# A spectral mixer and a low-rank MLP mixer on one core: output stores of 128 rows, V by broadcast loads, px two pairs ahead

## The chip, the cores and the metric

The kernel runs on one core of a Trainium2 chip. The metric is the device time of one execution in microseconds (us). Four compute engines work side by side, each through its own instructions in order: TensorE (PE in the profile, its weight loads PEld), VectorE (DVE), ScalarE (ACT) and GpSimd (POOL). SyncE (SP) only issues transfers. Transfers are issued here from POOL's queue and from SP's queue, and all of them are carried by 16 DMA engines.

## The reference

The input `x` has 8 batches of 3136 rows with 256 channels. Cut to what matters:

```python
X = np.fft.rfft(x, axis=1)
y = np.fft.irfft(X * (filt_r + 1j * filt_i)[None], n=3136, axis=1)   # global filter over the rows
yt = y.transpose(0, 2, 1)
u = y + (yt @ U @ V).transpose(0, 2, 1)          # U: 3136 x 32, V: 32 x 3136
out = u + np.maximum(u @ w_ch1, 0.0) @ w_ch2     # 256 -> 1024 -> 256, for every row
```

Inputs and output are float32. Inside, the kernel works in float16 with float32 sums.

## The kernel before, in words

**The transform.** 3136 = 64 x 49, so a row number is 49 q + r. The Fourier transform over q (64 points) is a product with the matrix `w64`, the one over r with the tables `t2`. What comes out of `t2`, the tile `px`, is multiplied by the filter tile `ft`; the tables `g12` take the result back over r, giving the spectrum `e2` over q alone, which stays as it is until the MLP needs it. The work of one batch in the middle stage is 16 pairs m of 64-row frequency groups: `forward` (L382) makes `px`, `both_products` (L390) or `product` (L401, L403) multiplies by the filter into `uv`, and a third step goes back over r.

**Batch 0** takes a way of its own, without DRAM in the middle: `first_f1` (L255 to L271), `first_a` (L283, L285) and `first_mid` (L294 to L337). In the loop of `first_mid`, pair m's `px` is made right before its product; the PSUM tag "m", from which it takes its bank, has 4 banks. At the loop's first round of a quarter, `swap_filters` (L188, L189) copies a quarter of the filter to the other half of the partitions and negates the imaginary part. After the loop, transposes (L328) fill `e2`, and between them run the first steps of batch 1, `f1_units`.

**Batches 1 to 7** go through DRAM between the steps. `f1_units` (L348) multiplies a chunk of `x` by `w64` and copies it to a tile `asb`, of which there are 3; each chunk is stored to `c1` (L358) by two transfers, from SP for batch 1 and from POOL for the others. `load_a` (L367) reads it back by frequency, `stream` runs the 16 pairs and stores `esb` to `c2` (L424), and `load_e` (L374) reads that into `e2`.

**The low rank part.** `U` and `V` are brought into the kernel's order. V is loaded in `load_v` (L210) by four loads that each fill 32 partitions of a constant tile `vq`; `prep_v` (L215) reorders it to `vr` by two GpSimd copies. `h1_unit` (L449) makes U's product `ph`, copied to `h1` (L453). `make_u` (L471, L476, L501) then adds V's product and brings the spectrum back to rows.

**The MLP and the output.** Rows are dealt with in groups: a group is up to 4 values of r, each with 128 rows (64 of r and 64 of r + 25). Each batch has 6 groups of 4; the values r = 24 of two batches share one short group, with one value, after every odd batch. `mm1` (L508) and `mm2` (L529, L533) are the two layers of a group, and mm2 of a group runs beside mm1 of the next. DVE copies the sums to the output tile `och` (L538), of which there are 2, two values of r at a time. After a group's last copy, two stores of 64 partitions each go to the output from POOL's queue (L545).

**What sets the order.** The order on every engine is the order in which the program writes its instructions. A table `sched` written out by hand (`put`, `run`) names slots in the groups' sequence at which the steps of later batches are written between the matmuls; a batch takes 48 slots, two for each quarter of a group of 4. Tiles of one tag share a given number of buffers: the writer of a tile waits until the tile that held its buffer before is read. Each new load of `x` waits for one of 8 `xt` buffers.

Of the kernel before, what the change touches and what calls it, by code (L numbers as in the profile page):

```python
# [9 lines left out]
F16 = mybir.dt.float16  # L10
F32 = mybir.dt.float32
RELU = mybir.ActivationFunctionType.Relu

SEQ = 3136
NQ, NR = 64, 49
NS = 32
DM = 256
RANK = 32
ESC = 16.0
NH = 25  # L20
CH = [6, 6, 6, 7]
# [64 lines left out]
def kernel(  # L86
# [40 lines left out]
    def rows(ap, b, o, n, np_=NQ):  # L127
        return bass.AP(tensor=ap.tensor, offset=ap.offset + b * SEQ * DM + o,
                       ap=[[RD, np_], [1, n]])
# [65 lines left out]
        load_filters(a, b)  # L195
    uq = sb.tile([64, NR * RANK], F16, tag="esb", bufs=2, name="uq")
    nc.gpsimd.dma_start(uq, moe_U.rearrange("(q r) p -> q (r p)", q=NQ))
    vq = cst.tile([128, SEQ], F16)
    w1 = cst.tile([128, 2 * 1024], F16)
    nc.gpsimd.dma_start(w1, moe_w_ch1.rearrange("(h dd) c -> dd h c", h=2))  # L200
    w2 = cst.tile([128, 8 * DM], F16)
# [3 lines left out]
    vr = cst.tile([128, NH * 128], F16)  # L205
    usb = cst.tile([128, NH * RANK], F16)

    def load_v():
        for j in range(4):
            nc.gpsimd.dma_start(vq[32 * j:32 * j + 32, :], moe_V)  # L210

    def prep_v():
        for h in range(2):
            w = NH - h
            nc.gpsimd.tensor_copy(  # L215
                vr.rearrange("p (r h q) -> p h r q", h=2, q=NQ)[:, h, 0:w, :],
                vq.rearrange("p (q r) -> p r q", r=NR)[:, h * NH:h * NH + w, :])

    def new_e2(b):
        e2 = sb.tile([128, NH * DM], F16, tag="e2", bufs=2, name="e2")  # L220
# [53 lines left out]
    def first_a(m):  # L274
        gi, ml = divmod(m, KG // 2)
        if ml == 0:
            st[0].setdefault("a", {})[gi] = sb.tile([98, KG * DM], F16, tag="a2", bufs=4, name="a2")
        pt = bank("o", "pt")
        for sl in range(2):
            for dh in range(2):  # L280
                o = sl * DM + dh * 128
                k = dh * 64 * NR + (2 * m + sl) * 98
                nc.tensor.matmul(pt[0:98, o:o + 128], at[:, k:k + 98], idn[:, :],  # L283
                                 start=True, stop=True, skip_group_check=True)
        nc.scalar.copy(st[0]["a"][gi][:, ml * 512:(ml + 1) * 512], pt[0:98, :])  # L285


    def first_mid(fill):

        et = sb.tile([128, 2 * NH * 128], F16, tag="e2", bufs=2, name="et")  # L290
        etv = et.rearrange("p (e r h k) -> p h e r k", e=2, h=2, k=64)
        pend = None

        def back(m, uv):  # L294
            pi = bank("fx"[m % 2], "pi")
            for sl in range(2):
                for dh in range(2):
                    for fi in range(2):
                        g = (4 * m + 2 * sl + fi) * 98
                        o = fi * 512 + sl * DM + dh * 128  # L300
                        a = (dh * 2 + sl) * 98
                        nc.tensor.matmul(pi[:, a:a + 98], uv[:, o:o + 128], g12[:, g:g + 98],
                                         start=(fi == 0), stop=(fi == 1), skip_group_check=True)
            for h in range(2):
                nc.scalar.copy(
                    etv[:, h, :, 0:NH - h, 4 * m:4 * m + 4],
                    pi[:, 0:392].rearrange("p (e k r) -> p e r k", e=2, r=NR)
                    [:, :, h * NH:h * NH + NH - h])

        for m in range(NS // 2):  # L310
            if m % 4 == 0 and m:
                swap_filters(*PARTS[m // 4])
            uv = both_products(m, forward(m, st[0]["a"][m // 4], ("m",)))
            if pend is not None:
                back(*pend)
            pend = (m, uv)
            if m + 2 < NS // 2:
                first_a(m + 2)
        back(*pend)
        e2 = new_e2(0)  # L320
        for n0 in range(0, NH, 2):
            pt = bank("m", "pe")
            w = min(2, NH - n0)
            k = 64 if w == 1 else 128
            for rr in range(w):
                for dh in range(2):
                    o, a = rr * DM + dh * 128, (dh * NH + n0 + rr) * 128
                    nc.tensor.matmul(pt[0:k, o:o + 128], et[:, a:a + k], idn[:, :],  # L328
                                     start=True, stop=True, skip_group_check=True)
            dst = e2[0:k, n0 * DM:(n0 + w) * DM]  # L330
            if n0 % 4:
                nc.scalar.copy(dst, pt[0:k, 0:w * DM])
            else:
                nc.vector.tensor_copy(dst, pt[0:k, 0:w * DM])
            if n0 == 6:
                prep_u()
            next(fill)  # L337

    def f1_units(b, both):
        ne = 0  # L340
        for c in range(len(CH)):
            xt = st[b]["x"].pop(c)
            asb = sb.tile([128, 7 * DM], F16, tag="asb", bufs=3, name="asb")
            for n0 in range(0, CH[c], 2):
                w = min(2, CH[c] - n0) * DM
                k = 64 if c0[c] + n0 == NH - 1 else 128
                pf = bank("m", "pf")
                nc.tensor.matmul(pf[0:k, 0:w], w64[0:k, 0:k], xt[0:k, n0 * DM:n0 * DM + w],  # L348
                                 start=True, stop=True)
                dst = asb[0:k, n0 * DM:n0 * DM + w]  # L350
                if both and ne % 2:
                    nc.vector.tensor_copy(dst, pf[0:k, 0:w])
                else:
                    nc.scalar.copy(dst, pf[0:k, 0:w])  # L354
                ne += 1
                if n0 + 2 >= CH[c]:
                    for h, o, n in span(c0[c], c0[c + 1]):
                        (nc.sync if b == 1 else nc.gpsimd).dma_start(c1[b].ap()[:, o:o + n], asb[64 * h:64 * h + 64, 0:n])  # L358
                yield
# [17 lines left out]
    def forward(m, a2, xtags):  # L377
        ml = m % (KG // 2)
        px = bank(xtags[m % len(xtags)], "px")
        for sl in range(2):  # L380
            s = 2 * m + sl
            nc.tensor.matmul(px[:, sl * DM:(sl + 1) * DM], t2[:, s * 128:(s + 1) * 128],  # L382
                             a2[:, (2 * ml + sl) * DM:(2 * ml + sl + 1) * DM],
                             start=True, stop=True, skip_group_check=True)
        return px

    def both_products(m, px):
        uv = sb.tile([128, 1024], F16, tag="uv", bufs=3, name="uv")
        fap = ft[:, 2 * m * DM:2 * (m + 1) * DM]
        nc.vector.tensor_mul(  # L390
            uv.rearrange("p (f e) -> p f e", f=2),
            bass.AP(tensor=px.tensor, offset=px.offset, ap=[px.ap[0], [0, 2], [1, 512]]),
            bass.AP(tensor=fap.tensor, offset=fap.offset,
                    ap=[fap.ap[0], [NS * DM, 2], [1, 512]]))
        return uv
# [121 lines left out]
    def mm2(gx, rr):  # L517
        if gx < 0 or rr >= groups[gx][2]:
            return
        b, r0, nr = groups[gx]  # L520
        w = nr * 128
        if rr == 0:
            ochs[gx] = sb.tile([128, 4 * DM], F32, tag="och", bufs=2, name="och")
        if rr % 2 == 0:
            pos[gx] = bank("o", "po")
        po, ut, och = pos[gx], uts[gx], ochs[gx]
        o = (rr % 2) * DM
        for t in range(8):
            nc.tensor.matmul(po[:, o:o + DM], hs[gx, t][:, rr * 128:(rr + 1) * 128],  # L529
                             w2[:, t * DM:(t + 1) * DM], start=(t == 0), stop=False,  # L530
                             skip_group_check=True)
        for dh in range(2):
            nc.tensor.matmul(po[:, o + dh * 128:o + (dh + 1) * 128],  # L533
                             ut[:, dh * w + rr * 128:dh * w + (rr + 1) * 128], idn[:, :],
                             start=False, stop=(dh == 1), skip_group_check=True)
        if rr % 2 or rr == nr - 1:
            a = (rr - rr % 2) * DM
            nc.vector.tensor_copy(och[:, a:(rr + 1) * DM], po[:, 0:(rr + 1) * DM - a])  # L538
        if rr == nr - 1:
            for h in range(2):  # L540
                if nr == 1:
                    dst = rows(out, b - 1 + h, r0 * DM, DM)
                else:
                    dst = rows(out, b, (h * NH + r0) * DM, nr * DM)
                nc.gpsimd.dma_start(dst, och[64 * h:64 * h + 64, 0:nr * DM])  # L545

    sched = {}

# [13 lines left out]
    for part in PARTS[1:]:  # L562
        load_tables(*part)
    swap_filters(*PARTS[0])
    first_a(0)
    first_a(1)
    for b in (1, 2):
        for c in range(len(CH)):
            load_x(b, c)
        if b == 1:  # L570
            load_v()
    fill = f1_units(1, True)
    first_mid(fill)
    prep_v()
    next(h1_unit(0))
    make_u(0)

# [72 lines left out]
```

## Time and profile before

| | us |
|---|---|
| median of 3 runs (575.88 to 576.89) | 576.33 |
| the profiled execution | 578.7 |
| its span, from the first instruction to the last | 576.7 |
| TensorE busy in it | 529.6 |
| DVE, ACT, POOL busy | 371.3, 359.8, 250.7 |

The mean granted TensorE clock was 0.976. How to read the profile: a group line gives the source line, engine, operation, and written and read tile, with the count, the busy time and the mean; in the timeline a line begins with its start from the span's beginning and its duration, and the bracket at its end is the engine's idle time just before it and what ended that. In the DMA view a queue's line gives its packets, megabytes and the time its packets took as a share of 16 engines' time; an issue line gives the count, the size of each and the median time from issue to landing. A packet here is one contiguous piece that a DMA engine moves, or one of the small end marks that tell of a transfer's end. All times of steps come from the one profiled execution.

### The profile page before, as it was taken

How to read it: one execution, taken by the hardware profiler on the slowest of the kernel's cores; microseconds unless marked ns; L12 is line 12 of the kernel's file. 1: busy time of each engine (PE TensorE's matmuls, PEld its weight loads, DVE VectorE, ACT ScalarE, POOL GpSimd, SP SyncE). 2: the span in 40 equal slices, each digit the busy share in tenths (PEclk: the TensorE clock that was granted, in tenths of full speed). 3: DMA queues.
4: the chain of work that ended last, by engine and by line, in shares of the span. 5: the costliest groups of instructions: out<-in, count | busy, mean ns of one | idle time of the engine just before them, and what ended most of it. 6: DMA issues, size and time to landing. Idle time of an engine off the chain costs nothing.

```text
span 576.7 us, 11509 instructions
## 1 busy us (share of the span) xinstructions
PE 529.6 (92%) x4403; PEld 376.4 (65%) x4403; DVE 371.3 (64%) x544; ACT 359.8 (62%) x723; POOL 250.7 (43%) x356
## 2 busy tenths in 40 slices
PE   3666899999999999999999999999999899999990
PEld 3553467767677767767676767777777577677770
DVE  7886276766777577767777578767777477233440
ACT  3566656667667586667677686777665466644430
POOL 6546340254556456455555455454443443110111
PEclk9989799999999999999999999999999899999996
DMA  8999758876978857677879857777564654512221
GB/s 153 216 184 223 212 129 179 179 194 149 201 189 207 186 132 165 157 192 199 185 169 206 210 123 185 170 159 206 133 166 108 155 116 98 130 42 70 73 73 47
DMA packets 68150, 90.40 MB, mean 157 GB/s; under 512 B 6728, under 2 KB 53224, under 8 KB 67200
## 3 DMA queue, kind: packets, MB, share of 16 engines
q0 software_dynamic: 19664, 51.88, 40.9%
q1 hardware_dynamic: 48432, 37.81, 26.8%
q8 instruction: 34, 0.56, 0.4%
q14 instruction: 20, 0.16, 0.1%
HBM read 57.99 MB, written 48.17 MB: 184 GB/s over the span
## 4 chain that ended last, share of the span: by engine, by line
PE 80%; DVE 2%; ACT 2%; DMA 1%; issue 1%; POOL 0%; POOLq 0%; DVEq 0%; ACTq 0%
PE po L529 29%; PE phh L508 28%; PE pi L418 5%; PE px L382 4%; PE pu L471 4%; PE po L533 4%; PE pu L476 4%; PE pf L348 2%; ACT h L515 2%; DMA out_dram<-och 1%; DVE uv L403 1%; PE ph L449 1%; DVE uv L401 1%; DVE uv L390 0%; POOL out_dram L545 0%
## 5 line engine op out<-in xcount | busy, mean ns | idle before, releaser
L515 ACT ACTIVATE h<-phh 128x512 f16<-128x512 f32 (+1 forms) x350 | 186.6, 575 | 108.0 <-PE phh L508 107.5
L529 PE MATMUL po<-w,h 128*128 128x256 f16 x1568 | 203.2, 273 | 0.0
L508 PE MATMUL phh<-ut,w 128*128 128x512 f16 x768 | 198.5, 380 | 0.4 <-ACT ut L501 0.2
L406 POOL TENSOR_TENSOR y<-uv 128x512 f16<-128x512 f16 x96 | 110.3, 1149 | 150.8 <-DVE uv L403 76.8
L529 PEld LDWEIGHTS <-h 128*128 128x128 f16 x1568 | 150.1, 98 | 35.7
L403 DVE TENSOR_TENSOR uv<-px,ft 64x512 f16<-64x512 f32 x192 | 132.1, 688 | 2.6
L538 DVE COPY och<-po 128x512 f32<-128x512 f32 (+1 forms) x100 | 68.1, 681 | 88.5 <-PE po L533 79.6
L508 PEld LDWEIGHTS <-w 128*128 128x128 f16 x832 | 75.2, 98 | 53.0 <-issue 3.3
L545 POOL DMA_DIRECT2D out_dram<-och x104 | 55.8, 540 | 113.3 <-DVE och L538 103.5
L401 DVE TENSOR_TENSOR uv<-px,ft 128x512 f16<-128x512 f32 x96 | 66.0, 688 | 56.0 <-PE px L382 49.7
L422 ACT CAST esb<-pi 98x512 f16<-98x512 f32 x112 | 65.8, 588 | 43.2 <-PE pi L418 35.5
L382 PE MATMUL px<-a,t 98*128 98x256 f16 x256 | 51.2, 282 | 5.7 <-DVE uv L403 4.3
L354 ACT CAST asb<-pf 128x512 f16<-128x512 f32 (+1 forms) x79 | 44.9, 569 | 17.8 <-PE pf L348 15.7
L501 ACT CAST ut<-pu 128x512 f16<-128x512 f32 x96 | 52.0, 597 | 4.8 <-PE pu L476 4.5
L533 PE MATMUL po<-idn,ut 128*128 128x128 f16 x384 | 52.8, 219 | 0.0
L513 DVE TENSOR_SCALAR h<-phh 128x512 f16<-128x512 f32 (+1 forms) x66 | 42.9, 650 | 14.3 <-PE phh L508 13.8
L390 DVE TENSOR_TENSOR uv<-px,ft 128x1024 f16<-128x1024 f32 x32 | 38.5, 1221 | 10.2 <-PE px L382 9.8
L476 PEld LDWEIGHTS <-e 128*128 128x128 f16 (+1 forms) x400 | 31.7, 99 | 19.6 <-issue 4.7
L471 PE MATMUL pu<-vr,h 128*128 128x512 f16 (+1 forms) x112 | 40.6, 362 | 2.6 <-POOL vr L215 1.7
L476 PE MATMUL pu<-s,e 128*128 128x128 f16 (+1 forms) x400 | 41.2, 222 | 0.0
L533 PEld LDWEIGHTS <-ut 128*128 128x128 f16 x384 | 37.6, 98 | 4.4
L134 POOL DMA_DIRECT2D xt<-in_x_dram x64 | 34.3, 543 | 9.0 <-DMA w<-in_moe_w_ch_dram 3.6
(66 smaller groups left out, 348.1 us busy)
## 6 DMA issues: line engine op xcount, KB each, us to landing
out_dram<-och POOLq DMA_DIRECT2D x96, 256.0 KB, 4.2
a<-c SPq DMA_DIRECT2D x28, 392.0 KB
c<-esb SPq DMA_DIRECT2D x28, 392.0 KB
xt<-in_x_dram POOLq DMA_DIRECT2D x56, 192.0 KB, 6.2
c<-asb POOLq DMA_DIRECT2D x42, 192.0 KB, 3.2
e<-c SPq DMA_DIRECT2D x28, 200.0 KB
e<-c SPq DMA_DIRECT2D x28, 192.0 KB
xt<-in_x_dram POOLq DMA_DIRECT2D x8, 224.0 KB, 5.1
```

The source lines that it names most:

```text
L382: nc.tensor.matmul(px[:, sl * DM:(sl + 1) * DM], t2[:, s * 128:(s + 1) * 128], a2[:, (2 * ml + sl) * DM:(2 * ml + sl + 1) * DM], start=Tru ...
L401: nc.vector.tensor_mul(uv[:, 0:512], px[:, :], ft[:, a:a + 512])
L403: nc.vector.tensor_mul(uv[p:p + 64, 512:1024], px[q:q + 64, :], ft[q:q + 64, b:b + 512])
L406: nc.gpsimd.tensor_add(y, uv[:, 0:512], uv[:, 512:1024])
L422: nc.scalar.copy(esb[:, ml * 512:(ml + 1) * 512], pi[0:98, :])
L471: nc.tensor.matmul(pm[:, o:o + nr * k], h1[:, dh * 128:(dh + 1) * 128], vr[:, r0 * 128:r0 * 128 + nr * k], start=True, stop=False, skip_gr ...
L476: nc.tensor.matmul(pm[:, o + rr * k:o + (rr + 1) * k], e2[0:k, a:a + 128], s2[0:k, 0:k], start=False, stop=(rr == nr - 1), skip_group_chec ...
L508: nc.tensor.matmul(pm[:, 0:w], w1[:, dh * 1024 + t * 128:dh * 1024 + (t + 1) * 128], ut[:, dh * w:(dh + 1) * w], start=(dh == 0), stop=(dh ...
L515: nc.scalar.activation(h[:, 0:w], pm[:, 0:w], RELU)
L529: nc.tensor.matmul(po[:, o:o + DM], hs[gx, t][:, rr * 128:(rr + 1) * 128], w2[:, t * DM:(t + 1) * DM], start=(t == 0), stop=False, skip_gr ...
L533: nc.tensor.matmul(po[:, o + dh * 128:o + (dh + 1) * 128], ut[:, dh * w + rr * 128:dh * w + (rr + 1) * 128], idn[:, :], start=False, stop= ...
L538: nc.vector.tensor_copy(och[:, a:(rr + 1) * DM], po[:, 0:(rr + 1) * DM - a])
```

## The change

- **Stores.** A group's two stores of 64 partitions become one store of 128 partitions. Its DRAM side has the dimensions [2][64][row], its SBUF side is the tile's 128 partitions. Batches 0 to 6 issue it from POOL, the last batch from SP. The short group's tile is of a tag of its own, `ocho`, with one buffer.
- **V.** Two loads, one for each half of V's columns, each with a leading dimension of 4 with stride 0, fill 128 partitions. They use the two buffers of the tag `och`, which is free then, and the constant tile `vq` goes. They are issued before the loads of the MLP's weights, and the loads of x for batch 1 follow them directly. `prep_v` becomes 8 pieces of two copies, written before `first_mid`, with a load of x for batch 2 after every second one.
- **px.** In the loop of `first_mid` the `px` of pairs m + 1 and m + 2 are made before the product of pair m needs them, and `first_a` runs three pairs ahead instead of two.
- **asb.** It has 4 buffers instead of 3.

```diff
@@ loads at the start
-    vq = cst.tile([128, SEQ], F16)
+    vqs = [sb.tile([128, SEQ // 2], F16, tag="och", bufs=2, name="vq") for _ in range(2)]
+    for k in range(2):
+        nc.gpsimd.dma_start(vqs[k], bass.AP(
+            tensor=moe_V.tensor, offset=moe_V.offset + k * (SEQ // 2),
+            ap=[[0, 4], [SEQ, RANK], [1, SEQ // 2]]))
+    for c in range(len(CH)):
+        load_x(1, c)
     w1 = cst.tile([128, 2 * 1024], F16)
...
-    def load_v():
-        for j in range(4):
-            nc.gpsimd.dma_start(vq[32 * j:32 * j + 32, :], moe_V)
-
-    def prep_v():
+    def prep_v(k):
+        q0, n = 8 * k, 8
+        v = vqs[k // 4]
+        a = (q0 % (NQ // 2)) * NR
         for h in range(2):
             w = NH - h
             nc.gpsimd.tensor_copy(
-                vr.rearrange("p (r h q) -> p h r q", h=2, q=NQ)[:, h, 0:w, :],
-                vq.rearrange("p (q r) -> p r q", r=NR)[:, h * NH:h * NH + w, :])
+                vr.rearrange("p (r h q) -> p h r q", h=2, q=NQ)[:, h, 0:w, q0:q0 + n],
+                v[:, a:a + n * NR].rearrange("p (q r) -> p r q", r=NR)[:, h * NH:h * NH + w, :])
@@ first_mid
+        def ahead(m):
+            return forward(m, st[0]["a"][m // 4], ("m",))
+
+        pxs = [ahead(0), ahead(1)]
         for m in range(NS // 2):
             if m % 4 == 0 and m:
                 swap_filters(*PARTS[m // 4])
-            uv = both_products(m, forward(m, st[0]["a"][m // 4], ("m",)))
+            uv = both_products(m, pxs.pop(0))
             if pend is not None:
                 back(*pend)
             pend = (m, uv)
             if m + 2 < NS // 2:
-                first_a(m + 2)
+                pxs.append(ahead(m + 2))
+            if m + 3 < NS // 2:
+                first_a(m + 3)
@@ f1_units
-            asb = sb.tile([128, 7 * DM], F16, tag="asb", bufs=3, name="asb")
+            asb = sb.tile([128, 7 * DM], F16, tag="asb", bufs=4, name="asb")
@@ mm2
-            ochs[gx] = sb.tile([128, 4 * DM], F32, tag="och", bufs=2, name="och")
+            ochs[gx] = (sb.tile([128, 4 * DM], F32, tag="och", bufs=2, name="och") if nr > 1 else
+                        sb.tile([128, DM], F32, tag="ocho", bufs=1, name="ocho"))
...
-            for h in range(2):
-                if nr == 1:
-                    dst = rows(out, b - 1 + h, r0 * DM, DM)
-                else:
-                    dst = rows(out, b, (h * NH + r0) * DM, nr * DM)
-                nc.gpsimd.dma_start(dst, och[64 * h:64 * h + 64, 0:nr * DM])
+            o, step = ((b - 1) * SEQ, SEQ) if nr == 1 else (b * SEQ, NH)
+            dst = bass.AP(tensor=out.tensor, offset=out.offset + (o + r0) * DM,
+                          ap=[[step * DM, 2], [RD, NQ], [1, nr * DM]])
+            (nc.gpsimd if b < nb - 1 else nc.sync).dma_start(dst, och[:, 0:nr * DM])
@@ the order of the start
-    first_a(0)
-    first_a(1)
-    for b in (1, 2):
-        for c in range(len(CH)):
-            load_x(b, c)
-        if b == 1:
-            load_v()
+    for m in range(3):
+        first_a(m)
+    for k in range(8):
+        prep_v(k)
+        if k % 2:
+            load_x(2, k // 2)
     fill = f1_units(1, True)
     first_mid(fill)
-    prep_v()
     next(h1_unit(0))
```

## The prediction

> **What bounds the kernel now.** I read the page first, then the waits, then the timeline of three stretches (the start, one middle batch, the end), then the DMA view of short windows. The page:
>
> ```profile
> span 576.7 us, 11509 instructions
> PE 529.6 (92%) x4403; PEld 376.4 (65%) x4403; DVE 371.3 (64%) x544; ACT 359.8 (62%) x723; POOL 250.7 (43%) x356
> q1 hardware_dynamic: 48432, 37.81, 26.8%
> PE 80%; DVE 2%; ACT 2%; DMA 1%; issue 1%; POOL 0%; POOLq 0%; DVEq 0%; ACTq 0%
> ```
>
> TensorE carries the chain, so time can be won only where it stands idle: in the first 62 us, at a few short groups, and behind the last matmul. The timeline of the start shows which waits these are; the last bracket of a line is the idle time and what ended it:
>
> ```profile
> 42.81 2.36 DVE L390 TENSOR_TENSOR uv<-px,ft 128x1024 f16<-128x1024 f32 x2 [0.65 <-PE px L382]
> 56.42 0.69 DVE L352 CAST asb<-pf 128x512 f16<-128x512 f32 x1 [2.50 <-DMA c<-asb]
> 57.17 0.38 PE L348 MATMUL pf<-xt,w 128*128 128x512 f16 x1 [2.47 <-DVE asb L352]
> 61.30 0.58 PE L471 MATMUL pu<-vr,h 128*128 128x512 f16 x1 [1.74 <-POOL vr L215]
> ```
>
> Waits over 100 to 577 us, of DVE (first line) and over 66 to 577 us of PE (second): total, times, longest. These are the reuses of `och` after a short group:
>
> ```profile
> DVE och L538 <- DMA out_dram<-och: 5.5, 2, 3.5
> PE px L382 <- DVE uv L403: 4.3, 4, 2.7
> ```
>
> The stores of the output, from the timeline of batch 2 and of the end. The tile stored from 218.33 is written again at 231.46, two groups on; the last batch stores every 8.3 us:
>
> ```profile
> 218.33 1.09 POOL L545 DMA_DIRECT2D out_dram<-och  x2
> 231.46 0.69 DVE L538 COPY och<-po 128x512 f32<-128x512 f32 x1
> 542.58 1.06 POOL L545 DMA_DIRECT2D out_dram<-och  x2 [7.21 <-DVE och L538]
> 550.86 1.06 POOL L545 DMA_DIRECT2D out_dram<-och  x2 [7.21 <-DVE och L538]
> 563.62 2.11 POOL L545 DMA_DIRECT2D out_dram<-och  x4 [3.77 <-DVE och L538]
> ```
>
> The DMA view of two windows, 480.4 to 483.6 us (one `c2` store alone; first line) and 500 to 540 us (ten half stores, nothing else large), and one short stretch of the windows view (its last two numbers are the share of 16 DMA engines and GB/s):
>
> ```profile
> q1 hardware_dynamic: 798, 0.40, 45.6%
> q0 software_dynamic: 800, 2.62, 26.7%
> out_dram<-och POOLq DMA_DIRECT2D x10, 256.0 KB, 3.6
> 378.95:379.15 0.20, 0.20 (x4) 0.19 (x3) 0.20 (x1) 0.00 (x0) 0.20 (x2) 1.00 0.91 369
> ```
>
> **How a DMA is dealt out.** The `c2` store is 98 rows of 8 pieces: 784 pieces of 512 B, and 798 packets, so 14 end marks. 784 pieces would divide by 16; 98 rows divide by 14. So on SP's queue the outermost count sets how many of the 16 engines work. The ten half stores on POOL's queue give 640 rows and 160 marks, 16 each: 64 rows on 16 engines. The new store has a DRAM side of [2][64][row]: outermost count 2 against SBUF's 128. No row shows two sides that differ; the bounds are 2 engines and 16. I take 2, by the 98-row line: a split has to fit both sides. The V loads lead with a stride-0 count of 4, so I take 4 engines there.
>
> The Trainium skill speaks on both sides. "DMA: Bandwidth & Descriptors", "Rules for kernel authors", advises one 128-partition transfer instead of two halves. The same section warns that an outermost count under 16, a leading stride-0 broadcast above all, confines a DMA to that many engines; its section on the semaphore increment of 16 adds that SP's queue then always takes the lowest-numbered engines, POOL's a rotating set. By the first rule alone the sum would be that of the first rival, 568; by the second, the forecast's.
>
> **One store on two engines.** 512 KB is 262 KB an engine. Best rate: 369 GB/s at 0.91 of 16 engines is 25.3 GB/s, so 10.4 us. Mean rate of the last batch: 2.62 MB in 26.7% of 16 x 40 us is 15.3 GB/s, so 17.1 us. A half store lands 3.6 us after issue, of which its data takes 262 KB / (16 x 15.3) = 1.1; the fixed part is 2.5. Issue to landing: 12.9 to 19.6 us, where it was 3.6.
>
> **The change, part by part.**
>
> *px two pairs ahead.* The product's idle time ended by px is 0.65, 0.28, 0.65, 0.28, 0.65. The first 1.86 cannot be kept: the third quarter of the imaginary filter, issued at 19.54, landed 13.4 us later at 32.9, just as L189 read it (32.93). Gain 0.65 (0 to 2.5).
>
> *Fourth `asb`.* TensorE's 2.47 before 57.17 goes: 2.4. Next late is the accumulation of `ph`, as before.
>
> *V.* The 1.74 before 61.30 ends at the earliest point if `vr` is done early; `h1` is ready at 59.99 (59.60 and 0.39), so 1.3 of the wait is V's alone. With 0.65 and 2.4 that makes 4.4 on 16 engines. On 4 engines: 20 to 40 us ran at 205 GB/s and a share of 1.19, 10.8 GB/s an engine; a V half of 401 KB takes 9.3 us instead of 2.3, so, issued near 29 behind a queue that took `uq` 10.2, it lands near 48. POOL then has 7.04 us of copies in 16 pieces and 8 x loads at 0.54 between them, 11.4 in all; queued behind are the memsets of `e2` and `usb`, for which `ph` waits. `ph` near 60, `pu` near 61.6: the gain is eaten (+0.3). I take -1 for the start; ends -4.4 and +2. The x loads of batch 2 (needed from 65) are covered: x(2,0) issues near 50 and landings took 8 to 11.
>
> *Short groups' own tile.* Takes away the 5.5 us of `och` waits; TensorE saw at most 0.7 + 0.7 + 2.7 of them. Worth 2.7 if stores stay quick (0 to 4.1); with slow stores it lies inside the next item.
>
> *Halved issues on POOL.* 46 x 0.54 us freed on an engine at 43%: nothing.
>
> *Stores of batches 0 to 6.* Issue to reuse is 231.46 - 218.33 = 13.1 us. Batch 0 runs slower groups and is covered. Alone a store takes 12.9: no wait. SP's queue uses 26.8% of all engine time (32.6% between 100 and 500), so 10.4 / (1 - 0.326) = 15.4, landing after 17.9. I take 15, between. DVE then waits 1.9 at the reuse; behind it stand the products, hence px's only bank. Some 0.7 is absorbed; the rest stalls TensorE. Each wait also delays the next store, so it comes once in two groups: 18 times over 36 groups, 18 x 1.2 = 22 us (0 at 12.9; 18 x 4.1 = 74 at 17.9). I assume successive stores fall on different engine pairs, which no row shows.
>
> *`c1` stores queued behind them.* The last one of batch 4, at 222.28, landed in 3.2; a load followed at 227.5, px at 236.4. Some 5 us of slack against up to 10 of queueing: 3 us over five batches (0 to 10).
>
> *Last batch from SP.* SP has issued its last e load (497.6) before the first of these stores; nothing is queued behind their waits. If all six use the same pair, they queue: first issue 526.0, fixed 2.5, 6 x 10.4, the short store 65 KB / 25.3 = 2.6: landed at 593.5. Before, the last landed at 565.2 + 3.4 = 568.6. Cost 24.9 (were the pairs to differ: 563.4 + 12.9 = 576.3, so 7.7; at 15.3 GB/s: 66).
>
> Sum: -1 + 22 + 3 + 25 = +49. The profiled execution took 578.7 (span 576.7 and 2.0 around it), 2.4 over the median of 576.33; the difference applies to the median: 625.
>
> **The rivals.**
>
> 1. *16 engines: faster.* The row that 64-row stores use all 16 speaks for it, the 798 packets against. Start -4.4, short groups -2.7, tail: one issue on SP instead of four on POOL, landing near 567.3 instead of 568.6, -1.3. 568. It decides from 4 engines on: 524 KB / (4 x 25.3) + 2.5 = 7.7 us, under every reuse interval.
> 2. *Only SP's queue is confined; POOL spreads anyway.* The marks differ between the queues (14 against 16 a DMA). -4.4 - 2.7 + 24.9 = +18: 594.
> 3. *Two engines, and POOL's stores all on one pair.* 15.4 us a group instead of 10.4: over 36 groups +180, near 800.
>
> **How the numbers follow.** Forecast (two engines on both queues) 0.62, own range 598 (no waits in the middle, start -1) to 700 (74 and 10 instead of 22 and 3, the start at +2); rival 2: 0.15; rival 1: 0.17; rival 3: 0.04; gains and losses that cancel: 0.02. The range 590 to 695 takes in the forecast and rival 2. The measurement tells about 0.2% (1.2 us) from no change: faster 0.17, same 0.03, slower 0.80.
>
> **What would show it.** Right: 512 KB stores that land 13 us and more after issue; DVE's `och` copies waiting for DMA tens of times; DMA busy share near 2/16 in the last batch and 25 us of it behind the last matmul. Start: no idle time before `asb`, `vr` late or early by V's landing. Wrong: landings near 3 us (rival 1), or slow ones in the last batch alone (rival 2).

## The result, and the profile after

The changed kernel takes 718.38 us (median of 4 runs, 713.47 to 723.03) against 576.61 for the kernel before: a ratio of 1.2432, with a 95% interval from 1.2308 to 1.2556. The profiled execution took 721.3 us. The direction of the forecast held; the size did not: 142 us were lost where 49 were expected, and the time lies outside the range.

The page of the changed kernel, with the lines that answer to those shown of before:

```profile
span 719.5 us, 11454 instructions
PE 566.2 (79%) x4403; PEld 393.0 (55%) x4403; DVE 371.2 (52%) x544; ACT 363.0 (50%) x723; POOL 233.9 (32%) x309
q0 software_dynamic: 56416, 48.75, 32.5%
q1 hardware_dynamic: 49356, 41.08, 23.1%
DMA 43%; PE 31%; issue 6%; DVE 4%; POOL 2%; ACT 2%; SPq 0%; DVEq 0%; POOLq 0%; ACTq 0%
```

Two things stand out. The chain of work that ended last runs through transfers for 43% of the span, where TensorE had 80% of it before. And TensorE does the same 4403 matmuls in 566.2 us instead of 529.6.

Where the 142.8 us of span went, by the windows view of the two traces, cut at the first `make_u` of batch 0 and at the first store of the last batch:

| stretch | before | after | change |
|---|---|---|---|
| start, to the first `pu` with `vr` | 61.3 | 65.4 | +4.1 |
| middle, to the last batch's first store | 464.7 | 589.8 | +125.1 |
| last batch | 50.7 | 64.3 | +13.6 |

In the middle, TensorE was busy for 455.3 us before (62 to 526 us) and for 488.0 after (66 to 655), +32.7; its idle time rose from 8.7 to 101.0, +92.3. The waits of TensorE in that stretch (total, times, longest) and, in the last line, of DVE:

```profile
PE px L394 <- DMA a<-c: 61.5, 12, 9.8
PE phh L520 <- DVE h L525: 15.8, 8, 3.1
PE ph L461 <- DMA e<-c: 10.2, 2, 5.7
PE ph L461 <- issue: 5.1, 1, 5.1
PE pi L430 <- ACT esb L434: 3.9, 1, 3.9
DVE och L551 <- DMA out_dram<-och: 36.6, 10, 7.9
```

None of the five waits of TensorE was in the trace of before. The largest is not the wait for the output tile, whose trace on TensorE is the 15.8 us of `phh`, but the one for `load_a`: `px` of batches 1 to 7 stands still until the spectrum has come back from `c1`.

The store itself is as slow as forecast; this is its line in the DMA view (count, size, median us from issue to landing):

```profile
out_dram<-och POOLq DMA_DIRECT2D x42, 512.0 KB, 15.3
```

The chain of waits shows what the slow stores do to the others (start, duration, what):

```profile
91.32 15.92 DMA c<-esb
107.31 0.32 SPq L386
108.13 8.83 DMA a<-c
...
197.06 14.15 DMA c<-asb
211.33 8.81 DMA a<-c
```

These are a `c2` store, a `load_e` (L386), a `load_a`, a `c1` store and again a `load_a`. The first `load_a` does not need the data of that `c2` store: SP issues it behind the `load_e` that waits for the store. The stores are slower than before: `c1` stores from POOL landed in 3.2 us in the median (7.3 now), and SP's waits for the `c2` stores that `load_e` must follow came to 101.3 us in 28 waits (174.2 now, the longest 15.6 instead of 5.8).

Why a transfer of a few hundred KB takes 9 to 17 us can be read in the DMA view of a stretch in which one output store is in flight and `load_a` has only its last two engines left (169 to 174 us; packets, MB, share of 16 engines):

```profile
DMA packets 127, 0.27 MB, mean 55 GB/s; under 512 B 15, under 2 KB 70, under 8 KB 125
q0 software_dynamic: 55, 0.23, 10.9%
q1 hardware_dynamic: 71, 0.04, 3.1%
```

The 55 packets of POOL's queue are pieces of 4096 B (55 x 4096 = 0.225 MB). Of SP's 71, 15 are under 512 B and 55 more under 2 KB: the pieces of 512 B. So in 5 us as many small pieces went through as large ones, and in slices of 0.05 us from 170 to 172 us there are at most 2 large and 3 small in any one: on an engine that an output store holds, the two queues take turns, about a piece of the one and a piece of the other. A 4096-B piece takes 0.109 x 16 x 5 / 55 = 0.159 us. `load_a` is 784 pieces of 512 B, 56 an engine if it is dealt to 14 like the `c2` store of the same 98 rows; two engines let through 55 / (5 x 2) = 5.5 a us each, so the two shares that lie on the store's engines take 56 / 5.5 = 10 us, whatever the other engines do. The transfer is over when the slowest share is. This is near the 9 us of the loads shown above. The two longest, of 17.6 and 16.8 us (issued at 133.98 and 162.72), went out 0.4 us behind a `c2` store on the same queue, which has as many pieces of its own; at the same rate the two together would take 20 us (an estimate).

"DMA: Bandwidth & Descriptors" of the Trainium skill, section "Queues, rings and completion order", states that an engine goes round its queues in turn, a whole packet of typically 9 to 17 pieces at a time. The turns agree with this trace; batches of that length it does not show: the two queues' pieces came out in equal number, 55 and 55, and mixed within each fraction of a us.

After the long waits TensorE runs slowly. The windows view around the wait that ended at 117.0 us (TensorE idle for 6.1 us, then; behind the busy times stand the granted clock, the DMA share and GB/s):

```profile
117.00:121.00 4.00, 3.99 (x16) 2.44 (x17) 1.92 (x2) 1.18 (x2) 0.00 (x0) 0.50 0.62 121
121.00:130.00 9.00, 8.99 (x73) 6.75 (x71) 5.38 (x6) 6.08 (x12) 1.88 (x3) 0.99 0.43 89
```

16 matmuls in 4 us at a clock of 0.50, then 73 in 9 us at 0.99. After the wait of 9.0 us that ended at 151.75 the clock was 0.50 until 158. The trace has 11 idle stretches of TensorE over 3.4 us between 66 us and the end, the kernel before none in its middle, and a clock of 0.50 follows each. In slices of 1 us over the middle, TensorE's busy time times what the granted clock lacks of 1 adds up to 34.1 us, in the kernel before to 2.8: 31.3 of the 32.7 us are the clock. The Trainium skill's "TensorE: Matmul & The Clock Gate", section "HAM oscillation — how this bites in real kernels", states a rule for this: a gap of more than about 3.4 us drops the clock to half. The long gaps agree. But shorter ones were followed by 0.50 too: six of 2.1 to 3.2 us in the middle of the changed kernel, though not two others, of 2.4 and 3.2, and one of 2.75 us in the kernel before (the shortest of the six, then that one):

```profile
380.62 1.87 PE L520 MATMUL phh<-ut,w 128*128 128x512 f16 x4 [2.11 <-DVE h L525]
457.71 0.61 PE L382 MATMUL px<-a,t 98*128 98x256 f16 x2 [2.75 <-DVE uv L403]
```

The clock was 0.50 from 381 to 384 us in the one and from 458 to 460 in the other. So 3.4 us is no safe bound here.

**The start.** POOL waited 8.37 us for V ahead of the x loads, began V's copies at 48.68, and its last two x loads waited again, for the weights; the memsets came behind all of that (last bracket: idle time and what ended it):

```profile
44.80 0.51 POOL L134 DMA_DIRECT2D xt<-in_x_dram  x1 [8.37 <-DMA vq<-in_moe_V_dram]
48.68 2.36 POOL L221 COPY vr<-vq 128x200 f16<-128x200 f16 x4
63.00 1.04 POOL L134 DMA_DIRECT2D xt<-in_x_dram  x2 [2.05 <-DMA w<-in_moe_w_ch_dram]
64.50 0.40 PE L461 MATMUL ph<-e,usb 128*32 128x256 f16 x1 [6.56 <-POOL usb L232]
```

**The end.** Last matmuls and last stores of the two kernels. First the last TensorE line of before in the timeline, and, by source line, its closing instructions on POOL's queue (shortest, median, longest in ns; first and last start):

```profile
563.31 0.28 PE L533 MATMUL po<-idn,odd 128*128 128x128 f16 x2
```

```profile
L645 POOLq DRAIN  x3: 51/108/10940, 565.0 to 576.4; - x3
```

and then the last TensorE line of after, and from its DMA view SP's queue in 661 to 672 us, where only stores of the last batch run:

```profile
700.50 0.42 PE L546 MATMUL po<-idn,odd 128*128 128x128 f16 x2
```

```profile
q1 hardware_dynamic: 144, 0.58, 12.8%
```

12.8% of 16 engines is two of them: SP's six stores queue on one pair. Behind its last matmul the kernel before still ran 576.7 - 563.6 = 13.1 us, the changed one 719.5 - 700.9 = 18.6: only 5.5 more. In the kernel before the last output landed near 568.6, and what came after was a closing instruction of 10.9 us on POOL, which issues its last store at 565.7.

### The profile page after: what moved, and what is told of

It is laid out like the page before. It is cut to its first block, busy times and chain, and to the rows that moved or that the text cites. A ratio compares the mean times of both kernels' runs of the same rounds, so it can differ in the third digit from the quotient of the medians.

```text
span 719.5 us, 11454 instructions
## 1 busy us (share of the span) xinstructions
PE 566.2 (79%) x4403; PEld 393.0 (55%) x4403; DVE 371.2 (52%) x544; ACT 363.0 (50%) x723; POOL 233.9 (32%) x309
## 2 busy tenths in 40 slices
DMA packets 105826, 90.55 MB, mean 126 GB/s; under 512 B 44180, under 2 KB 90804, under 8 KB 104876
## 4 chain that ended last, share of the span: by engine, by line
DMA 43%; PE 31%; issue 6%; DVE 4%; POOL 2%; ACT 2%; SPq 0%; DVEq 0%; POOLq 0%; ACTq 0%
DMA out_dram<-och 14%; DMA a<-c 13%; PE po L542 10%; PE phh L520 10%; DMA c<-asb 7%; DMA c<-esb 6%; PE px L394 2%; DVE uv L415 2%; PE pi L430 2%; DMA e<-c 2%; PE pu L483 2%; PE pu L488 1%; POOL y L418 1%; PE po L546 1%; PE pf L360 1%
## 5 line engine op out<-in xcount | busy, mean ns | idle before, releaser
L520 PE MATMUL phh<-ut,w 128*128 128x512 f16 x768 | 207.6, 394 | 18.1 <-DVE h L525 17.7
L542 PE MATMUL po<-w,h 128*128 128x256 f16 x1568 | 213.0, 281 | 2.9 <-DVE och L551 2.9
L542 PEld LDWEIGHTS <-h 128*128 128x128 f16 x1568 | 154.9, 101 | 44.8 <-issue 6.7
L551 DVE COPY och<-po 128x512 f32<-128x512 f32 x96 | 66.4, 691 | 140.4 <-PE po L546 78.4
L520 PEld LDWEIGHTS <-w 128*128 128x128 f16 x832 | 77.7, 100 | 78.1 <-issue 30.8
L394 PE MATMUL px<-a,t 98*128 98x256 f16 x256 | 52.0, 288 | 65.2 <-DMA a<-c 61.5
L394 PEld LDWEIGHTS <-t 98*128 98x128 f16 x256 | 22.5, 101 | 84.8 <-issue 45.5
L556 POOL DMA_DIRECT2D out_dram<-och x42 | 35.0, 834 | 97.9 <-DVE och L551 96.2
L488 PEld LDWEIGHTS <-e 128*128 128x128 f16 (+1 forms) x400 | 33.4, 104 | 20.6 <-issue 7.5
L483 PE MATMUL pu<-vr,h 128*128 128x512 f16 (+1 forms) x112 | 43.2, 386 | 1.3 <-ACT h L465 0.5
L488 PE MATMUL pu<-s,e 128*128 128x128 f16 (+1 forms) x400 | 43.2, 229 | 0.0
## 6 DMA issues: line engine op xcount, KB each, us to landing
out_dram<-och POOLq DMA_DIRECT2D x42, 512.0 KB, 15.3
```

The source lines that it names most:

```text
L483: nc.tensor.matmul(pm[:, o:o + nr * k], h1[:, dh * 128:(dh + 1) * 128], vr[:, r0 * 128:r0 * 128 + nr * k], start=True, stop=False, skip_gr ...
L488: nc.tensor.matmul(pm[:, o + rr * k:o + (rr + 1) * k], e2[0:k, a:a + 128], s2[0:k, 0:k], start=False, stop=(rr == nr - 1), skip_group_chec ...
L520: nc.tensor.matmul(pm[:, 0:w], w1[:, dh * 1024 + t * 128:dh * 1024 + (t + 1) * 128], ut[:, dh * w:(dh + 1) * w], start=(dh == 0), stop=(dh ...
```

## The experiments

Theories: **(A)** the cause is the stores' two engines, and the rest of the change is worth a few us of gain; **(B)** another part (V, px ahead, the order at the start, four `asb`) carries the loss. Inside A it was then open by which wait the time is lost.

**Halves in the changed kernel.** All of the change but the [2][64] store; the last batch's halves go out from SP.

```diff
-            (nc.gpsimd if b < nb - 1 else nc.sync).dma_start(dst, och[:, 0:nr * DM])
+            for h in range(2):
...
+                (nc.gpsimd if b < nb - 1 else nc.sync).dma_start(dst, och[64 * h:64 * h + 64, 0:nr * DM])
```

> The changed kernel with one edit undone: each store is two stores of 64 partitions again, from the same queues (POOL, the last batch from SP). Two-engine theory (a store whose outermost count is 2 works on 2 of 16 DMA engines, and all the loss comes from that): the middle runs as before; the start keeps its loss of 4 us, the short groups' waits go (-2.7), the end comes earlier: about 570 us, stores landing in 3 to 5 us. Order theory (the loss sits in the V loads, the new order on POOL or the stores' move to SP): 690 us or more.

568.83 us, a ratio of 0.9854 [0.9814, 0.9894]. The stores' line in the DMA view:

```profile
out_dram<-och POOLq DMA_DIRECT2D x84, 256.0 KB, 4.4
```

One edit takes away 150 us: A holds, B falls. Besides their two engines the wide stores also bring many tiny packets (last section). These added no time to POOL's queue: its packets took 0.325 x 719.5 = 234 us of 16 engines in the changed kernel and 0.409 x 576.7 = 236 in the kernel before. No run has the one without the other. The rest of the change, the last batch's stores from SP among it, gains 8 us on the kernel before.

**The wide store alone, on either queue.** First the kernel before with the [2][64] store from POOL for batches 0 to 6, second with it in the other branch, from `nc.sync`, for the last batch only.

```diff
+            if b < nb - 1:
+                o, step = ((b - 1) * SEQ, SEQ) if nr == 1 else (b * SEQ, NH)
+                dst = bass.AP(tensor=out.tensor, offset=out.offset + (o + r0) * DM,
+                              ap=[[step * DM, 2], [RD, NQ], [1, nr * DM]])
+                nc.gpsimd.dma_start(dst, och[:, 0:nr * DM])
+            else:
-            for h in range(2):
+                for h in range(2):
...
```

> The kernel before with one edit alone: batches 0 to 6 store [2][64] in one transfer from POOL; the last batch stays with half stores from POOL. Two-engine theory: the middle's loss alone, 125 us, so about 700 us. Order theory: within 5 us of before, 576.

730.3 us, 1.2654 [1.2585, 1.2724]. POOL's wide stores alone bring the loss of the middle. It is larger than in the changed kernel, where the short groups do not share `och`; here they do, and TensorE waits behind them:

```profile
PE px L382 <- DVE uv L403: 31.9, 3, 11.4
```

So the own tile for short groups seems to be worth much once stores are slow; no run changes it alone.

> The kernel before with one edit alone: the last batch's stores are [2][64] in one transfer from SP. Two-engine theory: six stores of 10.2 us queue on one pair of engines; last batch 64.3 us instead of 50.7 as in the changed kernel, so about 590 us. If the width of a store does not matter: 576 or less.

592.78 us, 1.0264 [1.0213, 1.0314]: the wide stores from SP cost 16 us in the last batch, as expected.

**The last batch's halves from SP.** The kernel before, with `nc.sync` for `nc.gpsimd` in the last batch alone. The question is whether POOL's closing instruction sets the end.

```diff
-                nc.gpsimd.dma_start(dst, och[64 * h:64 * h + 64, 0:nr * DM])
+                (nc.gpsimd if b < nb - 1 else nc.sync).dma_start(dst, och[64 * h:64 * h + 64, 0:nr * DM])
```

> The kernel before with one edit alone: the last batch's half stores come from SP instead of POOL. Drain theory (POOL's closing drain, which in the trace of before runs from 565.0 to 575.9, waits some 10 us after POOL's last transfer issue and sets the end): the end comes 1 to 2 us after the last landing, about 568 to 569 us. Landing theory (the end follows the last landing by a fixed 8 us, as the prediction assumed): 575 to 576 us.

570.58 us, 0.9877 [0.9843, 0.9912]. The profiled execution has a span of 568.2 us; its last matmul in the timeline:

```profile
562.92 0.28 PE L533 MATMUL po<-idn,odd 128*128 128x128 f16 x2
```

5.0 us behind the last matmul instead of 13.1. POOL's closing instruction takes nearly as long as before (9.7 us), but now starts behind the stores of batch 6, where nothing waits for it:

```profile
L653 POOLq DRAIN  x3: 51/103/9700, 517.8 to 567.9; - x3
```

The same bytes in the same pieces end the kernel 8 us sooner after its last matmul (6 us in the medians) when POOL has no store to close.

**How a late piece costs: half the row, and the row cut in two.** If the turns of large and small pieces are what slows `load_a`, shorter pieces should help. Both kernels are the wide POOL store from above. The first stores only the first half of each row's elements in batches 0 to 6, so half of the output is left out there; the second stores all bytes by two stores, each of half a row.

```diff
+                for c in range(2):    # first kernel: range(1)
+                    n = nr * DM // 2
+                    dst = bass.AP(tensor=out.tensor, offset=out.offset + (o + r0) * DM + c * n,
+                                  ap=[[step * DM, 2], [RD, NQ], [1, n]])
+                    nc.gpsimd.dma_start(dst, och[:, c * n:(c + 1) * n])
```

> As the second experiment (730 us), but each wide store of batches 0 to 6 carries only the first half of its rows' elements (2 KB pieces instead of 4 KB, still 64 pieces on each of 2 engines); the other half of these groups' output is not stored. Alternation theory (on the pair's two engines the two queues take turns piece by piece, so each of an a load's 56 pieces of 512 B waits for one store piece, 159 ns at 4 KB): a store lands in 8 us, an a load needs 56 x (80 + 27) ns = 6 us instead of 10.4, a margin of some 5 us covers most of it: 580 to 600 us. If a store's cost were its issue, its 64 descriptors an engine or its end marks: 700 us or more, as with whole rows.

It took 619 and 625 us, a ratio of 1.0755 [1.0684, 1.0826], and 630 in a third execution. (Its profiled execution took 1390 us and is not read.) Half the bytes leave a loss of some 44 us (0.0755 x 578) of 153, more than was expected.

> As the second experiment, with all bytes stored: each wide store is cut by columns into two of 2 KB pieces. Rotation theory (POOL's queue gives successive stores successive pairs): four engines, each busy 5.2 us a store; 580 to 605 us, as the fifth experiment. If both fall on the same pair: 10.4 us a group as before, 64 pieces twice: 700 us or more.

688.8 us, 1.1935 [1.1859, 1.2012], over 80 us above the expectation. POOL's queue in this kernel, and its stores:

```profile
q0 software_dynamic: 57296, 52.18, 37.3%
out_dram<-och POOLq DMA_DIRECT2D x96, 256.0 KB, 10.7
```

The kernel with uncut wide stores has 56576 packets on this queue. 45 more stores bring 45 x 16 = 720 end marks, and 720 is all the difference: twice as many pieces made no more packets, so the 2 KB pieces travel two to a packet (a packet of this view is then not one contiguous piece, as said ahead of the prediction), and a small piece of SP that takes turns with such a packet would wait as long as before. The half-row kernel has 35024 packets on this queue, so fewer turns but no shorter ones; whether shorter ones help stays open. What the cut gained is the landing, 10.7 us instead of 15.2 (11.2 for the cut stores alone, without the last batch's halves).

**Taking the waits away one at a time.** The wide stores stay, and the order is changed so that one kind of wait goes. First `load_a` of the second to fourth quarters 8 slots earlier (on the wide POOL store):

```diff
-    put(t - (6 if b == 1 else 8), one(load_a, b, gi))
+    put(t - (6 if b == 1 else 8 if gi == 0 else 16), one(load_a, b, gi))
```

> As the second experiment (730 us), with the a loads of the second to fourth quarter of each batch issued 8 slots (some 8 us) earlier. If late a loads are the main cost (TensorE waits 61 us for them, 12 times, in the changed kernel's trace): those of three quarters in four vanish, 660 to 690 us. If the reuse of och or sheer bandwidth is the main cost: 720 us or more.

719.68 us, 1.2453 [1.2377, 1.253]: 10 us gained, 40 to 70 expected. `px` waits for `a` fell from 60.7 to 36.4 us, what is left being the first quarters of five batches and the last quarter of batch 1, whose loads the edit leaves where they were, but DVE's waits for `och` rose from 75.9 to 83.3, and before `ph` 30.4 us were idle instead of 15.3.

Next three `och` buffers in the changed kernel (three `asb`, no own tile for the short groups, to make room), alone and with the earlier `load_a`:

```diff
-            asb = sb.tile([128, 7 * DM], F16, tag="asb", bufs=4, name="asb")
+            asb = sb.tile([128, 7 * DM], F16, tag="asb", bufs=3, name="asb")
-            ochs[gx] = (sb.tile([128, 4 * DM], F32, tag="och", bufs=2, name="och") if nr > 1 else
-                        sb.tile([128, DM], F32, tag="ocho", bufs=1, name="ocho"))
+            ochs[gx] = sb.tile([128, 4 * DM], F32, tag="och", bufs=3, name="och")
```

> The changed kernel (718 us) with three och buffers; to make room asb has three again and short groups have no tile of their own. DVE's waits for och to be stored (50.8 us in the changed kernel, of which TensorE sees some 19) vanish. If the waits add up: about 695 us. If one kind of wait takes the place of the other, as the seventh experiment suggests (loads earlier, and the och waits grew to 83 us): 705 to 718.

712.25 us, 1.2325 [1.2294, 1.2356]. DVE's waits for the stores are all but gone (5.1 us, once), and the kernel gains 6 us: `px` waits for `a` rose from 61.5 to 80.4 us. The waits stand in for each other.

> The ninth experiment with the a loads of the second to fourth quarters 8 slots earlier as well. If the two kinds of wait only stood in for each other, removing both frees what neither freed alone: 640 to 660 us, with the first quarters' a loads (behind c1 stores that queue behind the wide stores; some 10 us in each of five batches) left over. If something else holds the middle (bandwidth, SP's order): 690 us or more.

699.23 us, 1.2084 [1.2035, 1.2132]; 640 to 660 were expected. Six waits of `px` are left, up to 16.0 us long, 57.9 together, and `ph` stands idle for 25.4.

Two more on top of this one. All `c1` stores from SP, to take them out of POOL's queue:

```diff
-    (nc.sync if b == 1 else nc.gpsimd).dma_start(c1[b].ap()
+    nc.sync.dma_start(c1[b].ap()
```

> The tenth experiment with the c1 stores of all batches issued from SP instead of POOL, so that they take turns with the wide stores' pieces instead of standing behind them in POOL's queue. Queue theory: the first quarters' a loads come some 5 us earlier in each of five batches: 15 to 30 us under the tenth experiment. If SP's order delays them as much: the same or more.

701.12 us, 1.2129 [1.2088, 1.2169]: no gain. `px` waits 34.9 us instead of 57.9, `ph` 48.4 (28.3 for `e`, 20.1 for `a`), because SP issues in order and now also waits for `asb` (94.8 us in 14 waits). And the first quarters' `load_a` 8 slots, the f1 steps and the x loads 9 slots earlier:

```diff
-    put(t - (6 if b == 1 else 8 if gi == 0 else 16), one(load_a, b, gi))
+    put(t - (6 if b == 1 else 8 if b == 2 and gi == 0 else 16), one(load_a, b, gi))
-    steps[NP * (b - 1)] - 49 + 3 * k, fill)
+    steps[NP * (b - 1)] - 58 + 3 * k, fill)
-    put(steps[NP * (b - 1)] - 68 + 10 * c, one(load_x, b, c))
+    put(steps[NP * (b - 1)] - 77 + 10 * c, one(load_x, b, c))
```

> The tenth experiment (699 us; three och buffers, a loads of later quarters 8 slots earlier) with the first quarters' a loads 8 slots earlier too, and the f1 units and x loads that feed them 9 slots earlier. In the tenth experiment's trace TensorE still waits 58 us before the first px of a batch (six times) and 25 us before ph (three times). Chain theory (each batch has two pairs of dependent transfers, c1 store and a load, c2 store and e load, and each of the four takes up to 10 us longer on the pair of engines that stores): the first kind goes, the second stays: 640 to 665 us. Bandwidth theory: 690 to 700.

701.64 us, 1.21 [1.201, 1.219]: no gain again. Its waits of TensorE:

```profile
PE px L394 <- DMA a<-c: 31.9, 9, 6.8
PE ph L461 <- issue: 31.1, 4, 9.7
PE ph L461 <- DMA e<-c: 22.1, 3, 9.3
```

26 us went from `px` and 28 came to `ph` (25.4 before, 53.2 now). The chain from the filter product over `esb`, the `c2` store and `load_e` to `ph` had little room to begin with: twice in the kernel before TensorE already stood idle for 1.0 us ahead of `ph`. Five kernels thus put the loss elsewhere without ending it; of the kernels run, only those with quicker stores end it.

**The start.** On the halves in the changed kernel: batch 0's memsets of `e2` and `usb` on DVE, so that they do not queue behind `prep_v`.

```diff
-        nc.gpsimd.memset(e2[64:128, (NH - 1) * DM:NH * DM], 0.0)
+        (nc.gpsimd if b else nc.vector).memset(e2[64:128, (NH - 1) * DM:NH * DM], 0.0)
-        nc.gpsimd.memset(usb[64:128, (NH - 1) * RANK:NH * RANK], 0.0)
+        nc.vector.memset(usb[64:128, (NH - 1) * RANK:NH * RANK], 0.0)
```

> The first experiment (568.8 us), with the clearing of e2's and usb's last rows for batch 0 on DVE instead of POOL, where it queues behind the eight pieces of V's reordering and the x loads. TensorE's 6.4 us wait before ph's last product goes; V's product then waits for vr, done near 60.1 instead of pu's start at 64.3: -4, so 564 to 566 us. If the memsets are not what holds ph: 569.

566.18 us, 0.9788 [0.9756, 0.982]. The wait of 6.4 us for `usb` is gone, and the next in line shows, 2.2 us for `vr`:

```profile
62.76 0.38 PE L483 MATMUL pu<-vr,h 128*128 128x512 f16 x1 [2.16 <-POOL vr L221]
```

Then V by eight loads of 32 partitions in place of the two broadcasts, on top of that:

```diff
-        nc.gpsimd.dma_start(vqs[k], bass.AP(
-            tensor=moe_V.tensor, offset=moe_V.offset + k * (SEQ // 2),
-            ap=[[0, 4], [SEQ, RANK], [1, SEQ // 2]]))
+        for j in range(4):
+            nc.gpsimd.dma_start(vqs[k][32 * j:32 * j + 32, :], moe_V[:, k * (SEQ // 2):(k + 1) * (SEQ // 2)])
```

> The eighth experiment (566.2 us; in its trace V's product waits 2.2 us for vr until 62.8) with V loaded by eight loads of 32 partitions instead of two broadcast loads whose leading count is 4. Two-engine theory, applied to V: a load of count 4 works on 4 engines and lands late; on 16 engines vr is ready some 3 us sooner and the wait goes: 563 to 564 us. If V's landing is set by the load of all DMA engines together, not by its 4: 566.

561.97 us, 0.9726 [0.9705, 0.9747]: the best kernel of the study, faster than both. V's loads land in 4.1 us instead of 13.9, and nothing is late at the start:

```profile
57.76 0.39 PE L483 MATMUL pu<-vr,h 128*128 128x512 f16 x1 [0.48 <-ACT h L465]
```

That is 3.5 us earlier than the 61.30 of the kernel before; the forecast had named 4.4 as the most that could be won there.

## Why the prediction was right on how the stores run and wrong on what they cost

**How a DMA is dealt out: right.** Two engines on both queues; 15.3 us from issue to landing where 15 was taken. The assumption that POOL's successive stores fall on different pairs held too: two stores issued at 246.4 and 251.1 us overlap, and all landings between 244 and 275 us lie in 13.4 to 16.5 us, which one shared pair could not do with 10.2 us of pieces (64 x 0.159) each. On SP, all on the same pair, as assumed. The skill's rule in "DMA: Bandwidth & Descriptors", "Rules for kernel authors", which prefers one 128-partition transfer to two halves, did not hold for this shape: 718.38 us against 568.83 for the same kernel with halves. The rule of the same section on the outermost count did. Rivals 1, 2 and 3 fall with this.

**Stores of batches 0 to 6: right in the sum, in part by luck.** 22 us were predicted, from 18 waits of DVE of 1.9 (34 us together) less what is absorbed. Measured in the middle: 36.6 us of DVE in 10 waits, 15.8 of TensorE ahead of `phh`. There were about half as many waits, each about twice as long; the two errors cancel on DVE, and TensorE lost a little less.

**"`c1` stores queued behind them": this step failed.** It gave 3 us (0 to 10). Measured: 61.5 us of `px` behind `load_a`, 16.0 of `ph` (10.2, 5.1 and 0.7 for `esb`, which before had 1.0) and 3.9 of `pi`, some 80. Three things were wrong in it. It priced one transfer of a chain of four: `c1` store and `load_a` come one after the other, and so do `c2` store and `load_e`, and each of the four is slow where it meets the busy pair, whereas only the `c1` store was thought to; and SP's order hangs a `load_a` on a `c2` store whose data it does not need. It thought of queueing behind a store on POOL's queue, but SP's transfers of small pieces suffer too, on their own queue, by taking turns with 4096-B pieces. And it compared one queueing delay with a slack of 5 us, where a chain such as 14.15 + 8.81 us uses up several times that. Halves (568.83) show that the stores are the cause; that the waits replace each other is shown by the five kernels that keep the wide stores and move the order or the buffers, 699 to 720 us. How much of a late `c1` store is queueing in POOL's queue and how much the turns on an engine was not separated. No kernel that keeps the wide stores also makes `c2` to `ph` shorter, so how far a better order alone could go stays open.

**Not priced at all: the clock.** +32.7 us of TensorE time in the middle. The prediction counted waits as lost time only and put the slow matmuls behind them at nothing; they add a third again (32.7 on 92.3).

**The tail: right in what happens, too dear by 11 us.** 24.9 predicted, 13.6 measured: 6.3 of `och` waits on TensorE (3.4 and 2.9), 2.0 of slower matmuls, 5.5 behind the last matmul. The step held the last landing at 568.6 to be what ended the kernel before. It was not: POOL's closing instruction ended 8 us later. Storing from SP wins these 8 us, shown by the halves from SP, and the wide stores cost from there: 592.78 against 570.58, 22 us, near the 24.9 of the step.

**The start: wrong by 5 us.** -1 predicted (-4.4 to +2), +4.1 measured. px ahead gave what was said: in the halves kernel the last steps of batch 0's loop come 0.8 us earlier, against 0.65. The wait for `asb` went. But POOL's memsets were thought to come through in time for `ph` near 60; they ended at 64.4. V's copies began at 48.7, close to the forecast's 48, but the 16 pieces took 9.4 us instead of the 7.04 of the two whole copies, and the last x loads waited 2.05 us for the weights. The two experiments on the start show both parts: the memsets' place cost 2.7 us (568.83 to 566.18), the broadcast 4.2 (566.18 to 561.97).

**The range.** Its two ends do not follow from the terms named beside them: 625 without the 22 and 3 is 600, not 598, and with 74, 10 and +2 in place of 22, 3 and -1 it is 687, not 700. The measured 718 lies outside either.

## What to carry to other kernels

Before two stores are joined, read the outermost count of both sides: a [2][64] side put 512 KB on two engines and made 4 us into 15, so keep the two stores, whose outermost count is 64. A transfer that is slow but not waited for can still cost more through others: here it slowed the loads of small pieces beside it, and the sum of the dependent transfers (store, load back, use), not each one, must be held against the slack. And look at what really ends the kernel: where it is the closing work of the queue that issued the last store, storing from another queue wins time without moving a byte faster.

## What the runs showed of the hardware that was not expected

- Where both queues were busy on two engines, pieces came out one for one (55 of 512 B to 55 of 4096 B in 5 us), so the queue of small pieces moved an eighth of the other's bytes.
- Stores of 2 KB pieces from POOL went as pairs: 720 more packets for 45 more stores, all of them end marks.
- A POOL store confined to two engines brings tiny packets with it: packets under 512 B rose from 6728 to 44180 between the two kernels, and to 43640 with the wide stores alone, which is 42 stores x 14 engines x 64 more, less the 720 end marks of the 45 transfers saved.
- POOL's closing instruction took 10.9 us after its last store (9.7 after the stores of batch 6 where SP issues the last ones); without stores of POOL in the last batch the end came 5.0 us behind the last matmul instead of 13.1.
- TensorE's clock was 0.50 for 4 to 6 us after idle times of 6 and 9 us, and for about 3 us after one of only 2.1 us.
